# Rows of the last product 8 partitions apart, one VectorE copy and one output DMA, in a decode block on one core

## Chip, cores and metric

The kernel runs on one core of one Trainium2 chip. The metric is the device time of one execution in microseconds (us), as the median of several runs. The profile's span is about 2 us shorter than the time, because the two have different starts and ends. Spans are compared with spans here, and times with times.

## The reference, cut to what matters

The reference is one decode step of a transformer block for four sequences (B = 4): layer norm, attention over the last 2048 positions of a K and V cache, then layer norm and a gated MLP, each with a residual sum.

```python
# x: (4, 1, 1024); k_cache, v_cache: (4, 4, 8192, 128); wq: (1024, 4096); wo: (4096, 1024)
# w1, w3: (1024, 3584); w2: (3584, 1024); everything in bf16
h  = x + attention(layernorm(x), k_cache[:, :, -2048:], v_cache[:, :, -2048:], wq, wo)
h2 = h + (silu(layernorm(h) @ w1) * (layernorm(h) @ w3)) @ w2      # output: (4, 1, 1024)
```

There are only four rows of activations, so nearly all of the work is reading 55.6 MB of weights and cache. The output has 8 KB.

## The kernel before

The last product, `h @ w2` plus the residual, is what the change touches. The 1024 output columns are cut into JG = 4 slices of CG = 256. Slice `j` is computed by column group `j` of the TensorE array, so that four matmuls run side by side. Its four rows, one per sequence, stand in PSUM partitions 32j to 32j+3. The other partitions of each group of 32 are not used.

```python
# B = 4, JG = 4, QD = 32, CG = 256, IF = 7, P = 128
ident_f = const.tile([P, P], FP32)
nc.vector.tensor_copy(out=ident_f[:], in_=ident[:])
...
# the residual h1 (rows 32j+b) is put into the accumulator by an identity matmul
nc.tensor.matmul(y2_ps[:], lhsT=ident_f[:], rhs=h1[:], start=True, stop=False, skip_group_check=True)
... # gate, up, transposes of the gated product into hg_ps
hgT = act.tile([P, IF, JG, B], BF16)
nc.vector.tensor_copy(
    out=hgT[:], in_=hg_ps[:].rearrange("p i (j x) -> p i j x", j=JG)[:, :, :, :B]
)
for jf in range(JG):
    w2_t = loaded["w2"][jf]          # the last tile comes in pieces of 4, 2 and 1 chunks
    for i in range(IF):
        for j in range(JG):
            nc.tensor.matmul(
                y2_ps[QD * j : QD * j + B, :],
                lhsT=hgT[:, i, jf, :],
                rhs=w2_t[:, i, j * CG : (j + 1) * CG],
                start=False, stop=(jf == JG - 1 and i == IF - 1), skip_group_check=True,
            )

res = act.tile([P, CG], BF16)
nc.vector.tensor_copy(out=res[:, : CG // 2], in_=y2_ps[:, : CG // 2])
nc.scalar.copy(out=res[:, CG // 2 :], in_=y2_ps[:, CG // 2 :])
for j in range(JG):
    q = nc.sync if j % 2 == 0 else nc.scalar
    q.dma_start(out=out_flat[:, j * CG : (j + 1) * CG], in_=res[QD * j : QD * j + B, :])
```

Of the kernel before, what the change touches and what calls it, by code (L numbers as in the profile page):

```python
# [10 lines left out]
P = 128  # L11
# [3 lines left out]
BF16 = mybir.dt.bfloat16  # L15
FP32 = mybir.dt.float32
# [3 lines left out]
def kernel(  # L20
# [13 lines left out]
    nc = tc.nc  # L34

    B, _, D = A_x.shape
# [15 lines left out]
    out_flat = out.flatten_outer_dims()  # L52
# [9 lines left out]
    const = ctx.enter_context(tc.tile_pool(name="const", bufs=1))  # L62
    act = ctx.enter_context(tc.tile_pool(name="act", bufs=1))
# [3 lines left out]
    JG = 4  # L67
    QD = P // JG
    CQ = Hq * Dh // JG
    CG = D // JG  # L70
    CF = F // JG
    HF = CF // 2
    IF = CF // P
# [83 lines left out]
    ident = const.tile([P, P], BF16)  # L157
# [6 lines left out]
    for j in range(JG):  # L164
        nc.scalar.dma_start(
            out=x_q[QD * j : QD * j + B, :], in_=x_flat[:, j * CG : (j + 1) * CG]
# [7 lines left out]
    for c in range(2):  # L174
# [8 lines left out]
        out=xn[:], in0=x_sb[:], scalar1=mv[:, 0:1], scalar2=rstd[:, 0:1],  # L183
# [12 lines left out]

    qz = act.tile([P, B, Hkv * QD + REP], BF16)
    nc.vector.memset(qz[:], 0.0)
    ident_f = const.tile([P, P], FP32)
    nc.vector.tensor_copy(out=ident_f[:], in_=ident[:])  # L200

    sel = const.tile([P, RPO, RPO, P // RPO], BF16)
    ident_r = ident[:].rearrange("p (m r) -> p r m", r=RPO)
# [5 lines left out]
    for j in range(2, JG):  # L209
        nc.vector.tensor_tensor(  # L210
            out=same[:, 0, :], in0=same[:, 0, :], in1=ident[:, j * QD : (j + 1) * QD], op=ALU.add
# [6 lines left out]
    for kc in range(KC):  # L218
        wq_t = loaded["wq"][kc // KPC]
        for hf in range(CQ // 512):  # L220
            for g in range(JG):
# [3 lines left out]
                    lhsT=xnT[:, kc, :],  # L225
                    rhs=wq_t[:, kc % KPC, c0 : c0 + 512],
                    start=(kc == 0),
                    stop=(kc == KC - 1),
# [7 lines left out]
    for r in range(REP):  # L236
        nc.tensor.transpose(out=qt_ps[:, r, :], in_=q_sb[:, r * Dh : (r + 1) * Dh], identity=ident[:])
    nc.vector.tensor_copy(
        out=qz[:, :, : Hkv * QD].rearrange("p b (g z) -> p b g z", g=Hkv)[:, :, :, :REP],
        in_=qt_ps[:].rearrange("p r (g x) -> p x g r", g=Hkv)[:, :B, :, :],  # L240
# [24 lines left out]
    for u, (b, n) in enumerate(units):  # L265
        k_v = loaded["k"][b][:].rearrange("p (j d) -> p j d", d=Dh)
        kT = ktpool.tile([P, NJ, P], BF16, tag="kT")
        for t in range(NJ // TB):
            kt_ps = psA.tile([P, TB, P], BF16, tag=f"kt{nt % 4}")
            for jj in range(TB):  # L270
                nc.tensor.transpose(  # L271
                    out=kt_ps[:, jj, :], in_=k_v[:, n * NJ + t * TB + jj, :], identity=ident[:]
# [23 lines left out]
        out=Pm[:].rearrange("q (c jq) -> q jq c", jq=NSB), in_=scores_ps[:].rearrange("q (jq c) -> q jq c", jq=NSB),  # L296
# [22 lines left out]
    for b in range(B):  # L319
        v_t = loaded["v"][b]  # L320
        for g in range(Hkv):
            for j in range(NK):
                nc.tensor.matmul(  # L323
                    OT_ps[:, b, g * REP : (g + 1) * REP],
                    lhsT=v_t[:, g, j, :],
                    rhs=PT_sb[:, j, g * QD + b * REP : g * QD + (b + 1) * REP],
                    start=(j == 0),
                    stop=(j == NK - 1),
# [10 lines left out]
    for hh in range(RPO):  # L339
        nc.vector.tensor_copy(  # L340
            out=o4[hh * MP : (hh + 1) * MP, :, :, :].rearrange("p h r b -> p r h b"),
            in_=o4_ps[hh * MP : (hh + 1) * MP, :, :, hh, :],
# [7 lines left out]
    y2_ps = psB.tile([P, CG], FP32, tag="y2")  # L350
# [4 lines left out]
    for h4 in range(Hq // RPO):  # L355
        wo_t = loaded["wo"][h4 * RPO // HPC]
        for r in range(RPO):
            for j in range(JG):
                nc.tensor.matmul(  # L359
                    y_ps[QD * j : QD * j + B, :],  # L360
                    lhsT=o4[:, h4, r, :],
                    rhs=wo_t[:, h4 % (HPC // RPO), r, j * CG : (j + 1) * CG],
                    start=(h4 == 0 and r == 0),
                    stop=(h4 == Hq // RPO - 1 and r == RPO - 1),
# [5 lines left out]
    h1 = act.tile([P, CG], FP32)  # L370
# [20 lines left out]
        out=hn[:], in0=h1[:], scalar1=tot[:, 0:1], scalar2=rstd2[:, 0:1],  # L391
# [5 lines left out]
    for r in range(KPC):  # L397
# [3 lines left out]
        out=hnT[:], in_=hn_ps[:].rearrange("p r (j x) -> p j r x", j=JG)[:, :, :, :B]  # L401
    )

    nc.tensor.matmul(y2_ps[:], lhsT=ident_f[:], rhs=h1[:], start=True, stop=False, skip_group_check=True)


    def gate_up(kind, out_ps):
# [26 lines left out]
    hg_ps = psB.tile([P, IF, P], BF16, tag="tp")  # L434
    hg_v = hg[:].rearrange("q s c -> q (s c)").rearrange("q (p i) -> q i p", i=IF)
    for i in range(IF):
        nc.tensor.transpose(out=hg_ps[:, i, :], in_=hg_v[:, i, :], identity=ident[:])
    hgT = act.tile([P, IF, JG, B], BF16)
    nc.vector.tensor_copy(
        out=hgT[:], in_=hg_ps[:].rearrange("p i (j x) -> p i j x", j=JG)[:, :, :, :B]  # L440
    )


    for jf in range(JG):
        w2_t = loaded["w2"][jf]
        for i in range(IF):
            for j in range(JG):
                nc.tensor.matmul(  # L448
                    y2_ps[QD * j : QD * j + B, :],
                    lhsT=hgT[:, i, jf, :],  # L450
                    rhs=w2_t[:, i, j * CG : (j + 1) * CG],
                    start=False,
                    stop=(jf == JG - 1 and i == IF - 1),
                    skip_group_check=True,
                )

    res = act.tile([P, CG], BF16)
    nc.vector.tensor_copy(out=res[:, : CG // 2], in_=y2_ps[:, : CG // 2])  # L458
    nc.scalar.copy(out=res[:, CG // 2 :], in_=y2_ps[:, CG // 2 :])  # L459
    for j in range(JG):  # L460
        q = nc.sync if j % 2 == 0 else nc.scalar
        q.dma_start(out=out_flat[:, j * CG : (j + 1) * CG], in_=res[QD * j : QD * j + B, :])


# [28 lines left out]
```

## Time and profile before

| | before |
|---|---|
| time, median of 3 runs | 140.18 us (139.8 to 140.3) |
| span of the profiled run | 137.7 us |
| read from HBM | 55.59 MB, 404 GB/s over the span |
| last w2 data landed | 133.94 us |

The first lines are from the page of the kernel before: the span, the row of the 40 slices for the DMA engines (each digit is the busy share in tenths), and the chain that ended last, by line.

```profile
span 137.7 us, 2361 instructions
...
DMA  5999999999999999999999999999999999999950
...
DMA 61%; PE 22%; ACT 10%; DVE 2%; issue 2%; ACTq 0%
DMA w_t<-in_B_w_dram 42%; DMA k_t<-in_A_k_cache_dram 14%; PE kt_ps L271 11%; DMA wq_t<-in_A_wq_dram 5%; ACT kT L277 5%; PE scores_ps L256 5%; PE OT_ps L323 4%; ACT Pm L295 3%; DVE rmax L290 2%; PE pt_ps L309 1%; ACT L295 1%; PE y_ps L448 1%
```

The DMA engines are busy throughout, and the chain is mostly DMA. A change of the last steps can therefore gain only behind the last landing of weights.

The next lines are the timeline of the kernel before from there on. The columns are start and duration in us, then engine, line, operation and operands. The brackets give the idle time before an instruction and what ended it.

```profile
133.37 0.99 PE L448 MATMUL y_ps<-w_t,hgT 128*4 128x256 bf16 x12 [0.20 <-DMA w_t<-in_B_w_dram]
133.98 0.09 PEld L448 LDWEIGHTS <-hgT 128*4 128x4 bf16 x3 [0.32 <-issue]
134.41 0.29 DVE L458 CAST res<-y_ps 128x128 bf16<-128x128 f32 x1 [13.44 <-PE y_ps L448]
134.74 0.27 ACT L459 CAST res<-y_ps 128x128 bf16<-128x128 f32 x1 [30.90 <-DVE res L458]
135.03 0.66 SPq L462 DMA_DIRECT2D out_dram<-res  x2
135.03 0.62 ACTq L462 DMA_DIRECT2D out_dram<-res  x2
```

The ScalarE cast waited for the VectorE cast ("<-DVE res L458"), although it copies other columns, so the two halves came one after the other. Each queue then issued two DMAs. What follows them is not in the timeline but in the trace's records of landings and of the semaphore waits of SyncE, listed here in us of the span. A landing is the moment at which one DMA engine's share of a transfer counts as arrived.

```
before: last w2 landing 133.94 | first output issue 135.03
        the four output DMAs landed at 136.27  136.46  136.64  136.83 | end 137.72
        SyncE's closing waits released at 136.29  136.47  136.66  136.84  136.90
```

- "to issue" is from the last weight landing to the start of the first output issue (1.09 us here);
- "to landing" is from there to the last output landing (1.79 us);
- "to end" is from there to the end of the span (0.90 us).

Together the tail is 3.78 us.

### The profile page before, as it was taken

To read this page: it belongs to the slowest core of one execution; us is meant where nothing else is said; L and a number is where in the kernel's file an instruction comes from. 1 tells how busy PE (TensorE), PEld (TensorE's weight loads), DVE (VectorE), ACT (ScalarE), POOL (GpSimd) and SP (SyncE) were. 2 spreads that over 40 slices of the span, in tenths; PEclk is the share of its full clock that TensorE was granted. 3 is DMA by queue.
4 is the path that set the end of the run, shared out by engine and by line. 5 is a ranking of instruction groups with operands and counts; after the bars stand their busy time and mean duration, and the time that the engine had idled before them with its cause. 6 is when DMAs were issued, how large, how long until landed. Compare 5 with 4: busy or idle time off the path is not lost.

```text
span 137.7 us, 2361 instructions
## 1 busy us (share of the span) xinstructions
PE 73.3 (53%) x1057; PEld 43.4 (32%) x1057; DVE 37.0 (27%) x71; ACT 29.4 (21%) x29; POOL 0.7 (1%) x6
## 2 busy tenths in 40 slices
PE   0152254499898989400595759382244422654370
PEld 0111011296565656100595636220011110222220
DVE  6610000242343434530500181600008930300000
ACT  1200000125473737359440000000041000000000
POOL 2000000000000000000000000000000000000000
PEclk9999999999999999965555558965555555555555
DMA  5999999999999999999999999999999999999950
GB/s 159 453 401 438 438 409 447 438 409 443 424 416 406 419 421 424 419 425 428 431 424 428 424 442 417 437 416 450 413 446 416 446 421 433 433 421 441 398 236 2
DMA packets 6449, 55.74 MB, mean 405 GB/s; under 512 B 516, under 2 KB 548, under 8 KB 2856
## 3 DMA queue, kind: packets, MB, share of 16 engines
q1 hardware_dynamic: 6384, 55.58, 95.8%
q8 instruction: 8, 0.13, 0.3%
q10 hardware_dynamic: 56, 0.02, 0.1%
q14 instruction: 1, 0.01, 0.0%
HBM read 55.59 MB, written 0.01 MB: 404 GB/s over the span
## 4 chain that ended last, share of the span: by engine, by line
DMA 61%; PE 22%; ACT 10%; DVE 2%; issue 2%; ACTq 0%
DMA w_t<-in_B_w_dram 42%; DMA k_t<-in_A_k_cache_dram 14%; PE kt_ps L271 11%; DMA wq_t<-in_A_wq_dram 5%; ACT kT L277 5%; PE scores_ps L256 5%; PE OT_ps L323 4%; ACT Pm L295 3%; DVE rmax L290 2%; PE pt_ps L309 1%; ACT L295 1%; PE y_ps L448 1%; ACT PT_sb L315 0%; DVE res L458 0%; ACT res L459 0%
## 5 line engine op out<-in xcount | busy, mean ns | idle before, releaser
L277 ACT COPY kT<-kt_ps 128x1024 bf16<-128x1024 bf16 x16 | 15.9, 1013 | 15.0 <-PE kt_ps L271 15.0
L271 PE MATMUL kt_ps<-ident,k_t 128*128 128x128 bf16 x256 | 18.5, 235 | 0.9 <-DMA k_t<-in_A_k_cache_dram 0.9
L271 PEld LDWEIGHTS <-k_t 128*128 128x128 bf16 x256 | 16.4, 106 | 6.1 <-issue 4.9
L275 DVE COPY kT<-kt_ps 128x1024 bf16<-128x1024 bf16 x16 | 11.1, 692 | 18.1 <-PE kt_ps L271 18.1
L223 PE MATMUL q_ps<-wq_t,xnT 128*4 128x512 bf16 x64 | 7.5, 620 | 11.1 <-DMA wq_t<-in_A_wq_dram 11.1
L414 PE MATMUL u_ps<-w_t,hnT 128*4 128x448 bf16 x64 | 6.7, 568 | 10.4 <-DMA w_t<-in_B_w_dram 10.4
L414 PEld LDWEIGHTS <-hnT 128*4 128x4 bf16 x128 | 3.8, 104 | 24.4 <-issue 23.7
L256 PE MATMUL scores_ps<-kT,qz 128*32 128x512 bf16 x64 | 9.9, 609 | 3.0 <-ACT kT L277 3.0
L448 PE MATMUL y_ps<-w_t,hgT 128*4 128x256 bf16 x112 | 7.0, 410 | 6.7 <-DMA w_t<-in_B_w_dram 6.6
L414 PE MATMUL g_ps<-w_t,hnT 128*4 128x448 bf16 x64 | 6.1, 527 | 5.7 <-DMA w_t<-in_B_w_dram 5.5
L323 PE MATMUL OT_ps<-PT_sb,v_t 128*128 128x8 bf16 x256 | 7.4, 168 | 2.0 <-issue 1.8
L323 PEld LDWEIGHTS <-v_t 128*128 128x128 bf16 x256 | 7.3, 104 | 2.2 <-issue 2.0
L223 PEld LDWEIGHTS <-xnT 128*4 128x4 bf16 x64 | 2.0, 106 | 15.8 <-issue 15.4
L459 ACT CAST res<-y_ps 128x128 bf16<-128x128 f32 x1 | 0.3, 266 | 30.9 <-DVE res L458 30.9
L309 PE MATMUL pt_ps<-Dm,Pm 128*128 128x128 bf16 x16 | 1.9, 311 | 9.3 <-DVE Dm L302 9.3
L448 PEld LDWEIGHTS <-hgT 128*4 128x4 bf16 x112 | 3.7, 111 | 9.9 <-issue 7.8
L359 PE MATMUL y_ps<-wo_t,o_954 128*4 128x256 bf16 x128 | 5.1, 337 | 1.7 <-DVE y_ps L349 1.7
L427 DVE RECIPROCAL eg<-eg 128x896 f32<-128x896 f32 x1 | 5.8, 5752 | 0.0
L233 DVE TENSOR_SCALAR q_sb<-q_ps 128x512 bf16<-128x512 f32 x1 | 0.7, 692 | 16.9 <-PE q_ps L223 16.9
L234 ACT ACTIVATE q_sb<-q_ps 128x512 bf16<-128x512 f32 x1 | 0.6, 597 | 20.8 <-DVE q_sb L233 20.8
L295 ACT ACTIVATE Pm<-scores_ps,nmax 128x2048 bf16<-128x2048 f32 x1 | 4.8, 4784 | 0.0
L309 PEld LDWEIGHTS <-Pm 128*128 128x128 bf16 x16 | 1.6, 146 | 9.8 <-ACT Pm L295 9.8
(73 smaller groups left out, 42.4 us busy)
## 6 DMA issues: line engine op xcount, KB each, us to landing
w_t<-in_B_w_dram SPq DMA_DIRECT2D x11, 1792.0 KB, 27.9
wq_t<-in_A_wq_dram SPq DMA_DIRECT2D x4, 2048.0 KB, 11.6
k_t<-in_A_k_cache_dram SPq DMA_DIRECT2D x4, 2048.0 KB, 19.3
v_t<-in_A_v_cache_dram SPq DMA_DIRECT2D x4, 2048.0 KB, 36.8
wo_t<-in_A_wo_dram SPq DMA_DIRECT2D x4, 2048.0 KB, 22.8
w_t<-in_B_w_dram SPq DMA_DIRECT2D x1, 1024.0 KB
w_t<-in_B_w_dram SPq DMA_DIRECT2D x1, 512.0 KB, 29.3
w_t<-in_B_w_dram SPq DMA_DIRECT2D x1, 256.0 KB
```

Source lines behind the costliest of these rows:

```text
L223: nc.tensor.matmul(q_ps[QD * g : QD * g + B, hf * 512 : (hf + 1) * 512], lhsT=xnT[:, kc, :], rhs=wq_t[:, kc % KPC, c0 : c0 + 512], start=( ...
L256: nc.tensor.matmul(scores_ps[QD * g : QD * (g + 1), n * 512 : (n + 1) * 512], lhsT=qz[:, b, g * QD : (g + 1) * QD], rhs=kT_v[:, g, :, :], ...
L271: nc.tensor.transpose(out=kt_ps[:, jj, :], in_=k_v[:, n * NJ + t * TB + jj, :], identity=ident[:])
L275: nc.vector.tensor_copy(out=kT[:, t * TB : (t + 1) * TB, :], in_=kt_ps[:])
L277: nc.scalar.copy(out=kT[:, t * TB : (t + 1) * TB, :], in_=kt_ps[:])
L295: nc.scalar.activation(out=Pm[:].rearrange("q (c jq) -> q jq c", jq=NSB), in_=scores_ps[:].rearrange("q (jq c) -> q jq c", jq=NSB), func=A ...
L309: nc.tensor.matmul(pt_ps[:, jj, :], lhsT=Pm[:, (jb * JPB + jj) * P : (jb * JPB + jj + 1) * P], rhs=Dm[:], start=True, stop=True)
L323: nc.tensor.matmul(OT_ps[:, b, g * REP : (g + 1) * REP], lhsT=v_t[:, g, j, :], rhs=PT_sb[:, j, g * QD + b * REP : g * QD + (b + 1) * REP], ...
L359: nc.tensor.matmul(y_ps[QD * j : QD * j + B, :], lhsT=o4[:, h4, r, :], rhs=wo_t[:, h4 % (HPC // RPO), r, j * CG : (j + 1) * CG], start=(h4 ...
L414: nc.tensor.matmul(out_ps[QD * j : QD * j + B, hf, :HF], lhsT=hnT[:, k2, r, :], rhs=w_t[:, r, c0 : c0 + HF], start=(k2 == 0 and r == 0), s ...
L427: nc.vector.reciprocal(out=eg[:], in_=eg[:])
L448: nc.tensor.matmul(y2_ps[QD * j : QD * j + B, :], lhsT=hgT[:, i, jf, :], rhs=w2_t[:, i, j * CG : (j + 1) * CG], start=False, stop=(jf == J ...
```

## The change

The intent is to let one engine copy the result and one DMA store it. For that the four rows of each slice are spread over the 32 partitions of their group: row `b` of slice `j` goes to partition 32j+8b. All 16 rows are then exactly 8 partitions apart, and one access pattern with a partition step of 8 reaches them. The spreading is done by zero columns in the stationary operand, which becomes 32 columns wide.

```diff
-    ident_f = const.tile([P, P], FP32)
-    nc.vector.tensor_copy(out=ident_f[:], in_=ident[:])
+    RS = QD // B
+    spread = const.tile([P, JG, B, RS], FP32)
+    nc.vector.memset(spread[:], 0.0)
+    nc.vector.tensor_copy(
+        out=spread[:, :, :, 0], in_=ident[:].rearrange("p (j x) -> p j x", j=JG)[:, :, :B]
+    )
+    hgT = act.tile([P, IF, JG, B, RS], BF16)
+    nc.gpsimd.memset(hgT[:], 0.0)
...
-    nc.tensor.matmul(y2_ps[:], lhsT=ident_f[:], rhs=h1[:], start=True, stop=False, skip_group_check=True)
+    nc.tensor.matmul(
+        y2_ps[:], lhsT=spread[:].rearrange("p j b s -> p (j b s)"), rhs=h1[:],
+        start=True, stop=False, skip_group_check=True,
+    )
...
-    hgT = act.tile([P, IF, JG, B], BF16)
     nc.vector.tensor_copy(
-        out=hgT[:], in_=hg_ps[:].rearrange("p i (j x) -> p i j x", j=JG)[:, :, :, :B]
+        out=hgT[:, :, :, :, 0], in_=hg_ps[:].rearrange("p i (j x) -> p i j x", j=JG)[:, :, :, :B]
     )
...
-                    y2_ps[QD * j : QD * j + B, :],
-                    lhsT=hgT[:, i, jf, :],
+                    y2_ps[QD * j : QD * (j + 1), :],
+                    lhsT=hgT[:, i, jf, :, :].rearrange("p b s -> p (b s)"),
...
-    nc.vector.tensor_copy(out=res[:, : CG // 2], in_=y2_ps[:, : CG // 2])
-    nc.scalar.copy(out=res[:, CG // 2 :], in_=y2_ps[:, CG // 2 :])
-    for j in range(JG):
-        q = nc.sync if j % 2 == 0 else nc.scalar
-        q.dma_start(out=out_flat[:, j * CG : (j + 1) * CG], in_=res[QD * j : QD * j + B, :])
+    nc.vector.tensor_copy(out=res[:], in_=y2_ps[:])
+    nc.sync.dma_start(out=out_flat.rearrange("b (j c) -> j b c", j=JG), in_=res[0:P:RS, :])
```

On the DRAM side the 16 rows are in the order (slice, sequence). A step of one slice is 512 bytes and a step of one sequence is 2048 bytes.

## The prediction

> **What bounds the kernel.** The stream from HBM. The page's slices show the DMA engines at 9 tenths or more in 37 of 40, 404 GB/s over a 137.7 us span; the chain that ended last is 61% DMA, and from 104.07 to 133.33 us it is the weight loads alone. The engines wait for data (PE 53% busy; in the last product it idles 6.6 us in five waits for weight tiles). The change moves the same bytes in, so only the tail can change.
>
> **The tail before** (timeline, landing records): the last w2 piece lands at 133.94; its four matmuls run 133.98 to 134.39; VectorE casts half the result 134.41 to 134.71 (291 ns); ScalarE casts the other half only then, 134.74 to 135.01 (266 ns). Splitting bought no overlap. That agrees with the Trainium skill, "PSUM — Partial Sum Buffer", section on bank collisions: two engines are kept from touching one bank and quadrant together, and both halves lie in one bank. SyncE and ScalarE then issue two output DMAs each, 135.03 to 135.69. They land one after another at 136.27, 136.46, 136.64, 136.83. The closing barrier fills the rest to 137.72 (0.89 us).
>
> **What the change does, costed.**
> 1. No ScalarE cast; VectorE casts 256 columns. From the same engine reading PSUM at 128 columns (291 ns) and 512 (692 ns), an estimate for 256 is 425 ns. Done at 134.84 instead of 135.01: -0.17 us, on the path.
> 2. One DMA instead of four. The first of four took 1.24 us from issue to its last landing; the others cost 0.56 us more. One DMA has 16 rows of 512 B, four per engine instead of one (a packet takes about 28 ns: 0.08 us more): about -0.45 us, on the path. The skill's "DMA: Bandwidth & Descriptors", section "Issuing engines are not separate DMA queues", says that two issuing queues save only issue time; the landings 0.19 us apart agree.
> 3. The last product's stationary operand becomes 32 columns wide instead of 4. Weight loads of 32 columns took 93 ns, of 4 columns 80 to 85 at the same clock: 10 to 25 ns, paid once behind the last landing. Each matmul still streams 256 columns and the four column groups still overlap (28 matmuls in 1.66 us); the 2.6 us waits between tiles would hide more.
> 4. At the start: about 0.2 us more on VectorE and a GpSimd memset of 896 columns (about 1 us; a 128-column one took 0.20). The first big matmul waits for wq until 8.06 us, its transposed input is ready at 6.03: off the path. The strided hgT copy (217 ns before) may grow by tens of ns, hidden behind the wait for the second w2 tile.
>
> **Sum:** -0.17 - 0.45 + 0.02 = -0.6 us, 0.4%, about the run-to-run spread (139.8 to 140.3). From 140.18 I predict 139.6 us, 139.0 to 140.2 eight times in ten. Faster by over 2%: 0.01; within 2%: 0.98; slower: 0.01.
>
> **What would show each step:** no ScalarE cast, a VectorE cast near 425 ns; one output issue, landing 1.25 to 1.35 us later; the last w2 landing still at 133.5 to 134.3; the last product's matmuls within 3% of 7.0 us busy; span near 137.1.
>
> **What would make it wrong:** the single DMA landing late (fewer engines, rows apart slowing its reads); wide operands breaking the overlap of the column groups (over 2 us per tile); a shift in the stream's rate, where 1% is worth 1.3 us, more than the whole change; GpSimd's memset delaying VectorE by over 2 us at the start.

## The result and the profile after

| | before | change |
|---|---|---|
| time, median of 6 runs each | 140.00 us (139.75 to 140.40) | 139.85 us (139.76 to 140.08) |
| ratio, 95% interval | | 0.9987 (0.9967 to 1.0007) |
| span of the profiled run | 137.7 us | 138.0 us |
| last w2 landing | 133.94 us | 134.21 us |
| to issue + to landing + to end | 1.09 + 1.79 + 0.90 = 3.78 us | 0.95 + 1.79 + 1.09 = 3.83 us |

Ratios here and below are the mean time of one kernel's runs over that of the other's of the same rounds, so they are not quite the ratio of the medians. Executions over 1.5% slower than the fastest of the same kernel are left out of the means. The interval holds 1: no change of time is shown. The measured median lies inside the predicted range, but so does the time before (140.00 us), so this would have come out with no gain at all. The predicted gain of 0.6 us is nowhere in the tail.

The same lines of the page, for the changed kernel:

```profile
span 138.0 us, 2358 instructions
...
DMA  5999999999999999999999999999999999999940
...
DMA 61%; PE 22%; ACT 10%; DVE 2%; issue 2%; ACTq 0%
DMA w_t<-in_B_w_dram 41%; DMA k_t<-in_A_k_cache_dram 14%; PE kt_ps L278 11%; DMA wq_t<-in_A_wq_dram 5%; ACT kT L284 5%; PE scores_ps L263 5%; PE OT_ps L330 4%; ACT Pm L302 3%; DVE rmax L297 2%; PE pt_ps L316 1%; ACT L302 1%; PE y_ps L457 1%
```

The stream is the same, as predicted. The end of the timeline of the changed kernel:

```profile
133.62 1.04 PE L457 MATMUL y_ps<-w_t,hgT 128*32 128x256 bf16 x12 [0.20 <-DMA w_t<-in_B_w_dram]
134.25 0.11 PEld L457 LDWEIGHTS <-hgT 128*32 128x32 bf16 x3 [0.32 <-issue]
134.71 0.42 DVE L467 CAST res<-y_ps 128x256 bf16<-128x256 f32 x1 [13.06 <-PE y_ps L457]
135.16 0.69 SPq L468 DMA_DIRECT2D out_dram<-res  x1
```

One cast of 0.42 us and one issue are there, but that one issue took 0.69 us, as long as two issues before. The records behind it:

```
change: last w2 landing 134.21 | output issue 135.16
        its shares landed at 136.22 (the engines without a share)  136.88  136.90  136.91  136.95 | end 138.04
        SyncE's closing waits released at 136.96  137.03  137.09  137.16  137.22
```

Two things are seen before any experiment.

First, the single DMA landed 1.79 us after its issue began, exactly as late as the last of the four DMAs before. Its first packet started 1.28 us after the start of the issue; before, it was 0.76 us. The four late landings agree with the Trainium skill, "DMA: Bandwidth & Descriptors", section "Why a DMA increments its semaphore by 16 and not by 1": the number of DMA engines used is the largest one up to 16 that divides the slowest dimension of both sides, here 16 rows and 4 slices, so 4 engines.

Second, before, the four landings released four of SyncE's five closing waits one by one, and only one was left behind the last landing. After the change the first of the waits is for the one DMA, and the other four follow it at 0.06 to 0.07 us each. That is why the end takes 1.09 us instead of 0.90.

### The profile page after: what moved, and what is told of

It is laid out like the page before. It is cut to its first block, busy times and chain, and to the rows that moved or that the text cites. A ratio compares the mean times of both kernels' runs of the same rounds, so it can differ in the third digit from the quotient of the medians.

```text
span 138.0 us, 2358 instructions
## 1 busy us (share of the span) xinstructions
PE 73.8 (53%) x1057; PEld 44.6 (32%) x1057; DVE 37.7 (27%) x72; ACT 29.1 (21%) x28; POOL 1.5 (1%) x7
## 4 chain that ended last, share of the span: by engine, by line
DMA 61%; PE 22%; ACT 10%; DVE 2%; issue 2%; ACTq 0%
DMA w_t<-in_B_w_dram 41%; DMA k_t<-in_A_k_cache_dram 14%; PE kt_ps L278 11%; DMA wq_t<-in_A_wq_dram 5%; ACT kT L284 5%; PE scores_ps L263 5%; PE OT_ps L330 4%; ACT Pm L302 3%; DVE rmax L297 2%; PE pt_ps L316 1%; ACT L302 1%; PE y_ps L457 1%; ACT PT_sb L322 0%; DVE res L467 0%; DVE Dm L309 0%
## 5 line engine op out<-in xcount | busy, mean ns | idle before, releaser
L457 PE MATMUL y_ps<-w_t,hgT 128*32 128x256 bf16 x112 | 7.1, 414 | 6.6 <-DMA w_t<-in_B_w_dram 5.8
L457 PEld LDWEIGHTS <-hgT 128*32 128x32 bf16 x112 | 4.5, 135 | 9.2 <-issue 7.3
L366 PE MATMUL y_ps<-wo_t,o 128*4 128x256 bf16 x128 | 5.3, 344 | 1.7 <-DVE y_ps L356 1.7
L366 PEld LDWEIGHTS <-o 128*4 128x4 bf16 x128 | 3.5, 105 | 3.5 <-DVE y_ps L356 2.0
```

What stands on the lines that cost most here:

```text
L366: nc.tensor.matmul(y_ps[QD * j : QD * j + B, :], lhsT=o4[:, h4, r, :], rhs=wo_t[:, h4 % (HPC // RPO), r, j * CG : (j + 1) * CG], start=(h4 ...
L457: nc.tensor.matmul(y2_ps[QD * j : QD * (j + 1), :], lhsT=hgT[:, i, jf, :, :].rearrange("p b s -> p (b s)"), rhs=w2_t[:, i, j * CG : (j + 1 ...
```

## The experiments

Twelve runs were made, and each was also profiled. The tail is the most exact measure of what happens behind the last landing: in two profiles of the changed kernel it came to 3.83 us both times, while times of the same kernel spread over some tenths of a microsecond. It doesn't see a shift of the landing itself. The table gives all runs; the sections after it say what each was for.

| run | issue, each (us) | to issue | to landing | to end | tail | time / before in the same rounds (us) | ratio (95%) |
|---|---|---|---|---|---|---|---|
| before | 0.27 to 0.34 | 1.09 | 1.79 | 0.90 | 3.78 | | |
| change | 0.69 | 0.95 | 1.79 | 1.09 | 3.83 | 139.85 / 140.00 | 0.9987 (0.9967 to 1.0007) |
| a0_change_again | 0.69 | 0.95 | 1.79 | 1.09 | 3.83 | 139.84 / 139.70 | 1.0010 (0.9996 to 1.0023) |
| e1_four_dmas | 0.60 to 0.76 | 0.95 | 2.79 | 0.90 | 4.63 | 140.43 / 139.78 | 1.0050 (1.0036 to 1.0064) |
| e2_linear_rows (wrong) | 0.59 | 0.95 | 1.81 | 1.09 | 3.84 | 139.87 / 139.78 | 1.0009 (0.9996 to 1.0021) |
| e3_two_dmas | 0.63, 0.67 | 0.95 | 1.90 | 1.09 | 3.94 | 140.13 / 139.78 | 1.0027 (1.0014 to 1.0039) |
| e4_copy_alone | 0.27 to 0.34 | 0.93 | 1.79 | 0.90 | 3.62 | 139.54 / 139.78 | 0.9982 (0.9970 to 0.9995) |
| e5_last_semaphore | 0.70 | 0.95 | 1.80 | 0.84 | 3.58 | 140.45 / 139.72 | 1.0052 (1.0038 to 1.0067) |
| e6_dense_rows (wrong) | 0.80 | 0.95 | 1.90 | 1.09 | 3.94 | 140.01 / 139.72 | 1.0019 (1.0007 to 1.0032) |
| e7_dense_linear (wrong) | 0.36 | 0.95 | 1.42 | 1.09 | 3.45 | 139.47 / 139.72 | 0.9981 (0.9968 to 0.9994) |
| e8_step_two (wrong) | 0.61 | 0.95 | 1.83 | 1.09 | 3.86 | 139.89 / 139.72 | 1.0012 (0.9999 to 1.0026) |
| e9_scalar_copy | 0.27 to 0.34 | 0.87 | 1.79 | 0.89 | 3.56 | 139.48 / 139.70 | 0.9991 (0.9978 to 1.0004) |
| e10_last_semaphore_late | 0.67 | 0.95 | 1.79 | 0.84 | 3.58 | 139.68 / 139.70 | 1.0000 (0.9987 to 1.0012) |
| e11_rows_four_apart | 0.60 to 0.75 | 0.94 | 2.78 | 0.90 | 4.62 | 140.48 / 139.71 | 1.0053 (1.0036 to 1.0069) |

"Wrong" marks results that were wrong; all others were correct. In e10 the tail is counted from the last landing of w2 at 134.05 us, since one of the extra loads landed after it.

### a0_change_again: is the first profile typical?

The changed kernel was run again without an edit.

> The changed kernel once more, unchanged, on the chip of this call, for a second profile and a better ratio. Tail from the last weight landing to the end 3.83 us as in its first profile (0.95 to issue, 1.79 to landing, 1.09 to close), against 3.78 before; ratio of times 0.998 to 1.002.

The tail was 3.83 us again, with the same three parts, and the ratio was 1.0010. The last w2 landing was 134.03 us instead of 134.21, so that moment moves by some 0.2 us from run to run, and most of the 0.27 us by which it was later in the first profile is not an effect of the change. A small part may be: the landing was at 133.94 to 133.98 us in the three profiles with the old layout (before, e4, e9) and at 133.98 to 134.21 us in the ten with rows apart (all others but e5), with medians of 133.95 and 134.03 us. This shift of some 0.08 us lies before the tail, and its cause stays open.

### e1_four_dmas: why is the one DMA as slow as four?

My first theory, SHAPE, was that the two strides of the DRAM side make the issue slow. This run takes the second stride away and keeps the rows 8 partitions apart.

```diff
-    nc.sync.dma_start(out=out_flat.rearrange("b (j c) -> j b c", j=JG), in_=res[0:P:RS, :])
+    for j in range(JG):
+        q = nc.sync if j % 2 == 0 else nc.scalar
+        q.dma_start(out=out_flat[:, j * CG : (j + 1) * CG], in_=res[QD * j : QD * (j + 1) : RS, :])
```

> The changed kernel, but its one output DMA cut into four of four rows each, two on SyncE and two on ScalarE as before; rows stay 8 partitions apart. Theory SHAPE (the single DMA is slow to issue because its DRAM side steps through two strides, slices and batches): each issue is back at 0.27 to 0.34 us, first landing about 1.25 us and last landing about 1.8 us after the first issue, closing part 0.9 us again. From the last weight landing to the end: 0.95 + 1.8 + 0.9 = 3.65 us, 0.13 under the kernel before. Rival ROWS (16 rows, four per DMA engine, cost it): the same here. Rival DISTANCE (rows 8 partitions apart are slow to fetch): packets and landings stay late, first landing 1.5 us or more after issue. Time: within 0.2% of the changed kernel, so the trace decides, not the clock.

SHAPE fell. These are the instructions that write or read the result tile, for the kernel before and then for this run. The numbers after "x2:" are the shortest, median and longest duration in ns.

```profile
L462 SPq DMA_DIRECT2D out_dram<-res x2: 276/306/337, 135.0 to 135.4; - x2
L462 ACTq DMA_DIRECT2D out_dram<-res x2: 274/291/308, 135.0 to 135.3; - x2
```

```profile
L470 SPq DMA_DIRECT2D out_dram<-res x2: 687/721/755, 135.0 to 135.8; - x2
L470 ACTq DMA_DIRECT2D out_dram<-res x2: 602/650/698, 135.0 to 135.7; - x2
```

The DRAM side, the number of rows and the queues are the same in the two kernels. Only the partitions of the rows differ: neighbours before, every eighth here. Each issue takes more than twice as long, each queue has two of them in a row, and the last landing comes 2.79 us after the first issue instead of 1.79. The time is 0.5% longer than before, which is outside its noise. The rival DISTANCE was right that the partition step costs, but not in how: the packets themselves are not slow (25 to 33 ns each before and after the change); it is the issue that takes longer.

### e2_linear_rows and e3_two_dmas: rows, strides or step?

In e2 the one DMA writes its rows in one stride of DRAM. The order of the output is then wrong.

```diff
-    nc.sync.dma_start(out=out_flat.rearrange("b (j c) -> j b c", j=JG), in_=res[0:P:RS, :])
+    nc.sync.dma_start(out=out_flat.rearrange("b (j c) -> (b j) c", j=JG), in_=res[0:P:RS, :])
```

> Wrong order of the result on purpose: one DMA of the same 16 rows, but its DRAM rows follow each other in one stride of 512 bytes. SHAPE: issue 0.33 us instead of 0.69, last landing 1.25 to 1.35 us after issue instead of 1.79, time about 0.4 us (0.3%) under the changed kernel. ROWS, as far as it means 16 rows to generate: issue stays at 0.69 (if it means four rows per engine it may fall too, since 16 rows can now be dealt to 16 engines; the landing count tells). DISTANCE: landing stays at 1.7 us or more. Reference comparison must fail.

In e3 two DMAs of eight rows each keep both strides and the step.

```diff
-    nc.sync.dma_start(out=out_flat.rearrange("b (j c) -> j b c", j=JG), in_=res[0:P:RS, :])
+    for k in range(2):
+        q = nc.sync if k == 0 else nc.scalar
+        q.dma_start(
+            out=out_flat[:, 2 * k * CG : 2 * (k + 1) * CG].rearrange("b (j c) -> j b c", j=2),
+            in_=res[2 * QD * k : 2 * QD * (k + 1) : RS, :],
+        )
```

> The changed kernel with two output DMAs of eight rows, one on SyncE, one on ScalarE, each still with two strides on the DRAM side. SHAPE: each issue still takes 0.6 to 0.7 us though it has half the rows, side by side; last landing about 1.8 to 2.0 us after issue, no gain over one DMA. ROWS: issue falls to about 0.45 to 0.5 us and the last landing to about 1.5 us. DISTANCE: no change of issue, landing as in the changed kernel.

In e2 the issue fell only from 0.69 to 0.59 us and the landing stayed at 1.81 us, although the 16 rows were now dealt to 16 engines (16 late landings in the records instead of 4). So four rows per engine were not the only cost either. In e3 half the rows took 0.67 and 0.63 us, so the issue does not scale with the rows. SHAPE happened to expect the numbers of e3 rightly, but e1 and e2 had already taken it down as the only cause.

### e6, e7 and e8: each cause alone

The partition step and the second DRAM stride were now tested apart. All three runs read the wrong partitions or write in the wrong order.

```diff
 e6_dense_rows    in_=res[0 : JG * B, :]              out "b (j c) -> j b c"     (16 neighbours, two strides)
 e7_dense_linear  in_=res[0 : JG * B, :]              out "b (j c) -> (b j) c"   (16 neighbours, one stride)
 e8_step_two      in_=res[0 : 2 * JG * B : 2, :]      out "b (j c) -> (b j) c"   (every second, one stride)
```

> Wrong result on purpose: the changed kernel, the one DMA reads 16 neighbouring partitions instead of every eighth; DRAM side with its two strides as in the change. My SHAPE theory fell in the first runs (four-row DMAs without a second stride took 0.60 to 0.76 us each when their rows lie 8 apart). New theory STEP (a partition step other than 1 on the SBUF side alone makes an issue slow): issue 0.28 to 0.40 us, first packet 0.76 us after issue, last landing 1.25 to 1.4. Rival EITHER (a second stride on the DRAM side or a step on the SBUF side, each sends the issue down the slow way; the 16-row linear one took 0.59 and the loads of the K cache with more dims took 0.6): issue 0.55 to 0.7 us, last landing 1.65 or more.

> Wrong result on purpose: neighbouring partitions and one linear stride of DRAM. STEP and EITHER both: issue 0.28 to 0.35 us, last landing about 1.25 to 1.35 us, 0.45 to 0.55 under the changed kernel; tail from last weight landing about 3.3 us; time about 0.35% under the changed kernel. Rival ROWS (16 rows are slow to issue however they lie): issue 0.55 or more, last landing 1.7 or more.

> Wrong result on purpose: 16 rows two partitions apart, one linear stride of DRAM. STEP: as with a step of 8, issue 0.59 us, last landing 1.8. Rival DISTANCE, as far as it means how far apart the rows lie: between the dense one and the one of 8, issue near 0.35 to 0.45 us.

The issue of the one DMA, from the instructions of the result tile, in the order e6, e7, e8:

```profile
L468 SPq DMA_DIRECT2D out_dram<-res x1: 795/795/795, 135.0 to 135.0; - x1
```

```profile
L468 SPq DMA_DIRECT2D out_dram<-res x1: 355/355/355, 135.0 to 135.0; - x1
```

```profile
L468 SPq DMA_DIRECT2D out_dram<-res x1: 612/612/612, 134.9 to 134.9; - x1
```

With the changed kernel and e2 this makes a square for one DMA of 16 rows of 512 bytes (issue / last landing after the start of the issue, us):

| | one DRAM stride | two DRAM strides |
|---|---|---|
| 16 neighbouring partitions | 0.36 / 1.42 (e7) | 0.80 / 1.90 (e6) |
| every second partition | 0.61 / 1.83 (e8) | |
| every eighth partition | 0.59 / 1.81 (e2) | 0.69 / 1.79 (change) |

EITHER was right in kind, though the 0.80 us of e6 is above its 0.55 to 0.7, and STEP as the only cause fell with e6. Each of the two alone makes the issue slow and moves the landing by about 0.4 to 0.5 us; both together cost no more than one. A step of 2 costs as much as a step of 8, so the distance does not matter. And 16 rows as such are cheap: e7 landed after 1.42 us, a little over the 1.25 to 1.35 expected and near the 1.32 us (1.24 + 0.08) that my prediction used for the change. Its time was 0.19% under before, about half of the gain that the change was meant to bring. What in the hardware makes the difference, these runs don't show.

One rival is left in the square: with one DRAM stride the rows went to 16 engines, with two strides to 4 (16 and 4 late landings), so the second stride never came alone. The loads of the kernel before settle this for the issue, and I could have read it before I predicted. These are the instructions of two of its lines: the K cache (two strides in DRAM over the rows) and the weights wq (one stride). Both load 128 rows of 16 KB, and both land on 16 engines. For the landing of the output the rival stays open.

```profile
L95 SPq DMA_DIRECT2D k_t<-in_A_k_cache_dram x4: 593/608/615, 8.0 to 10.0; - x4
```

```profile
L89 SPq DMA_DIRECT2D wq_t<-in_A_wq_dram x4: 328/406/424, 0.7 to 2.4; - x4
```

The number of strides is not a complete rule, however. The load of `x_sb` has four neighbouring partitions and one stride of 2 KB, and its issue took 0.55 to 0.58 us in every run; it is the first DMA that ScalarE issues, and no run tells whether that is why. The first V load has its second DRAM stride inside each partition's row; it took 0.59 to 0.61 us right behind the K loads, but 0.40 us in e5, where it came 1.6 us after them.

### e4_copy_alone and e9_scalar_copy: the copy without the rest

Here the kernel before keeps its layout and its four DMAs and takes only one copy.

```diff
-    nc.vector.tensor_copy(out=res[:, : CG // 2], in_=y2_ps[:, : CG // 2])
-    nc.scalar.copy(out=res[:, CG // 2 :], in_=y2_ps[:, CG // 2 :])
+    nc.vector.tensor_copy(out=res[:], in_=y2_ps[:])        # e4_copy_alone
+    nc.scalar.copy(out=res[:], in_=y2_ps[:])               # e9_scalar_copy
```

> The kernel before with one part of the change alone: VectorE copies all 256 columns, ScalarE none; four output DMAs as before. All theories: copy 0.42 us, issue starts 0.14 to 0.17 us earlier after the last weight landing than before (0.92 to 0.95 instead of 1.09), the rest as before (1.8 to the last landing, 0.9 to close): 3.63 us from the last weight landing to the end instead of 3.78. Time 0.1% under before, inside the noise of the clock.

> The kernel before with ScalarE copying all 256 columns and VectorE none; four output DMAs as before. From ScalarE's 266 ns at 128 columns and 597 at 512, an estimate for 256 is 376 ns, 0.05 under VectorE's 425. So the issue starts 0.88 us after the last weight landing and the tail is 3.57 us; time 0.1 to 0.2% under before, not to be told from the copy by VectorE alone.

The end of the timeline of e4, and then the copy in e9:

```profile
134.42 0.42 DVE L458 CAST res<-y_ps 128x256 bf16<-128x256 f32 x1 [13.44 <-PE y_ps L448]
134.88 0.66 SPq L461 DMA_DIRECT2D out_dram<-res  x2
134.88 0.62 ACTq L461 DMA_DIRECT2D out_dram<-res  x2
```

```profile
134.45 0.37 ACT L458 CAST res<-y_ps 128x256 bf16<-128x256 f32 x1 [30.56 <-PE y_ps L448]
```

Both came out as expected: 3.62 and 3.56 us of tail against 3.78. The copy is the part of the change that gains, and it needs no new layout. In time, e4 is 0.18% under before, with an interval that leaves 1 out. For e9 the medians say 0.16%, but one of its five runs took 139.95 us, and its interval holds 1. The two were not run in the same rounds, so which is better is not shown by time.

Why ScalarE waited for VectorE in the kernel before is not shown. The prediction put it down to the shared PSUM bank. Two other pairs of copies stand in the same trace:

```profile
24.46 0.69 DVE L233 TENSOR_SCALAR q_sb<-q_ps 128x512 bf16<-128x512 f32 x1 [16.86 <-PE q_ps L223]
25.18 0.60 ACT L234 ACTIVATE q_sb<-q_ps 128x512 bf16<-128x512 f32 x1 [20.82 <-DVE q_sb L233]
...
67.34 0.69 DVE L313 CAST PT_sb<-pt_ps 128x512 bf16<-128x512 f32 x1 [0.77 <-PE pt_ps L309]
67.77 0.59 ACT L315 CAST PT_sb<-pt_ps 128x512 bf16<-128x512 f32 x1 [1.69 <-PE pt_ps L309]
```

In the first pair the engines read two halves of 512 columns of one tile, `q_ps`, and ScalarE waited as well. In the second they read different tiles, and ScalarE began at 67.77 us, before VectorE ended at 68.03. So in this program the wait goes with a shared PSUM tile. Whether two half copies overlap when the halves are in two tiles was not run.

### e5_last_semaphore and e10_last_semaphore_late: the longer end

In these traces the DMAs take their completion semaphores in turn from eight numbers, and SyncE waits for them in a fixed order at the end. In the changed kernel the output DMA has the first in this order. Four more small loads, whose data nobody reads, give it the last one.

```diff
+    x_more = act.tile([B, 4, CG], BF16)
+    for j in range(4):
+        nc.scalar.dma_start(out=x_more[:, j, :], in_=x_flat[:, j * CG : (j + 1) * CG])
```

In e5 these lines stand at the start, behind the loads of `x_q`. In e10 they stand before `gate_up("w3", u_ps)` and are issued by SyncE, behind the last weight load.

> The changed kernel with four more small loads at the start, which are never read; they only shift the output DMA from the first of the semaphores that SyncE waits for at the end to the last. Theory CLOSE (the four staggered landings of before hid SyncE's other closing waits; a single landing on the first semaphore makes them follow it, 65 ns each): from the last landing to the end 0.83 to 0.90 us instead of 1.09, everything else as in the changed kernel. Rival (the closing part is 0.2 us longer because one DMA's landing is acknowledged later): stays at 1.09. Time 0.1% under the changed kernel at most.

> The mended form of the run with four more loads: in that one they stood at the start, one of them waited for the semaphore of the first weight load, and ScalarE with it, so that the first large product began 3.5 us later. Here they are issued behind the last weight load, when their semaphores are free. Theory CLOSE: first large product at about 8.1 us as in the changed kernel, last weight landing 134.0 to 134.3, closing part 0.84 instead of 1.09, tail 3.57 us; time 0.25 us (0.2%) under the changed kernel. If the closing part is 0.84 and the time does not move, the last landing has moved instead.

The closing part fell to 0.84 us in both, as CLOSE had it: in e10 SyncE's first four closing waits were released 0.88 to 1.07 us before the landing, and only one was left behind it. So the order of the waits costs 0.26 us (1.09 - 0.84, from unrounded values) in the changed kernel.

In time, e5 was 0.5% slower nevertheless. The lines of its timeline show what was delayed; the second fence has the weight loads of wq in the changed kernel:

```profile
2.67 5.61 ACTq L171 DMA_DIRECT2D x_more<-in_A_x_dram  x4
...
6.58 2.06 SPq L89 DMA_DIRECT2D wq_t<-in_A_wq_dram  x3
...
8.30 1.28 ACT L183 ACT_TABLE_LOAD   x1 [8.30 <-DMA wq_t<-in_A_wq_dram]
...
11.62 1.88 PE L234 MATMUL q_ps<-wq_t,xnT 128*4 128x512 bf16 x16 [0.27 <-DVE xnT L195]
```

```profile
0.73 2.17 SPq L89 DMA_DIRECT2D wq_t<-in_A_wq_dram  x4
```

Two things were late. The fourth extra load had to wait for the semaphore of the first weight load. ScalarE waited with it, its square root for the layer norm came late, and the first large product began at 11.62 instead of 8.08 us. And the extra loads had taken the next semaphores in turn: SyncE's second load of wq got that of an `x_q` load, waited for it and was issued at 6.58 instead of 1.18 us. The last w2 landing moved by 0.75 us, from 134.21 to 134.96. The late weight loads suffice for that: in the first 12 us the DMA engines moved 323 instead of 351 GB/s, 0.34 MB less, which at the 432 GB/s of the changed kernel from 12 to 30 us is an estimated 0.78 us. That the late product adds to it is not shown. In e10 the first product began at 8.11 us and w2 landed at 134.05. Its median was 139.68 us, against 139.84 for the changed kernel of the same rounds; the intervals of their ratios to before overlap, so a gain is shown by the tail (0.25 us) and only suggested by the time (0.16 us).

### e11_rows_four_apart: the step once more, and a copy that tripled

Two open points: whether a step of 4 behaves like the others, and why VectorE's strided copy of `hgT` grew from 217 to 652 ns. The rows were put 4 partitions apart; the zero columns fill the stationary operand to 32 columns as before, so only the distance of the writes changes.

```diff
 against e1_four_dmas:
-    RS = QD // B
-    spread = const.tile([P, JG, B, RS], FP32)
+    RS, RB = 4, QD // 4
+    spread = const.tile([P, JG, RB, RS], FP32)
-        out=spread[:, :, :, 0], ...
+        out=spread[:, :, :B, 0], ...
-    hgT = act.tile([P, IF, JG, B, RS], BF16)
+    hgT = act.tile([P, IF, JG, RB, RS], BF16)
-        out=hgT[:, :, :, :, 0], ...
+        out=hgT[:, :, :, :B, 0], ...
-        q.dma_start(out=out_flat[:, j * CG : (j + 1) * CG], in_=res[QD * j : QD * (j + 1) : RS, :])
+        q.dma_start(out=out_flat[:, j * CG : (j + 1) * CG], in_=res[QD * j : QD * j + B * RS : RS, :])
```

> The run with four DMAs of four rows, with the rows 4 partitions apart instead of 8; the stationary operand stays 32 columns wide. Two questions. (1) Issue: if any step other than 1 sends it the slow way, each of the four issues again takes 0.60 to 0.76 us and the tail from the last weight landing is 4.6 us; if distance matters, less. (2) The strided copy of hgT, which grew from 217 to 652 ns (the prediction had tens of ns) when its writes came to stand 16 bytes apart: the Trainium skill, 'SBUF — State Buffer', section 'Specifications (TRN2)', speaks of 16-byte lines that need two hits each for full bandwidth. If that is it, writes 8 bytes apart take 220 to 260 ns; if any stride is slow, the copy stays near 650.

The issues took 0.60 to 0.75 us and the tail was 4.62 us: a step of 4 is as slow as one of 8. The copy of `hgT`, in the instructions of its tile, for the kernel before, the change and this run:

```profile
L439 DVE COPY hgT<-hg_ps x1: 217/217/217, 120.8 to 120.8; 128x112 bf16<-128x112 bf16 x1
```

```profile
L448 DVE COPY hgT<-hg_ps x1: 652/652/652, 121.0 to 121.0; 128x112 bf16<-128x112 bf16 x1
```

```profile
L448 DVE COPY hgT<-hg_ps x1: 392/392/392, 120.8 to 120.8; 128x112 bf16<-128x112 bf16 x1
```

The writes stand 2, 16 and 8 bytes apart. Neither expectation held: 8 bytes is between the other two, not at full speed. The lines of 16 bytes that the Trainium skill, "SBUF — State Buffer", section "Specifications (TRN2)", describes give the direction, since sparser writes are slower, but not the size; whether the lines are the reason, no run shows. None of this is on the critical path, because the next tile of w2 is waited for anyway.

## Why the prediction was right or wrong, point by point

**The bound and the verdict were right.** The stream takes the time up to about 134 us, nothing in the change moves it by more than about 0.1 us, and the time stays within 2%. The range held the median of 139.85 us, which took no insight: 139.0 to 140.2 us held the time before as well, and the largest term of the sum was wrong. Whether 139.85 is better than before at all is not shown: the ratios of the two measurements, 0.9987 and 1.0010, lie on both sides of 1.

**Step 1, the copy, was right.** "An estimate for 256 is 425 ns"; it took 424 ns. With the wide operand of step 3, the part up to the issue was to become 0.15 us shorter and became 0.14 us shorter (1.090 to 0.948). The ScalarE cast had waited for VectorE's before, and e4 shows that the copy alone gains 0.16 us of tail. The place in the Trainium skill that the prediction named, "PSUM — Partial Sum Buffer", section "PSUM bank collisions raise a hardware error", says that two engines must not meet in one bank and quadrant. The wait fits that, but ScalarE waited in the same way for the other half of `q_ps` (e4, above), so the bank is not shown to be its reason, and no run here let the two engines collide.

**Step 2, "one DMA instead of four", was wrong, and it was the largest term.** I took the first of four DMAs (1.24 us), added 0.08 us for its packets and wrote "about -0.45 us, on the path". It measured 0.00: 1.79 us before and after. The step that failed was the assumption that the new DMA is issued like the old ones. Its SBUF side steps by 8 partitions and its DRAM side has two strides, and the square of runs shows that with either of these the issue goes from 0.36 to 0.59 us or more and the landing from 1.42 to between 1.8 and 1.9 us. With neither of them (e7, whose result is wrong), 0.37 us of the expected 0.45 us are there. The list of what could go wrong had "rows apart slowing its reads": the step did matter, but in the issue and not in the reads.

**The closing part, "0.89 us", was treated as a constant and was not one.** It grew by 0.195 us, because the four landings, spread over 0.56 us, had let three of SyncE's five closing waits pass before the last landing, and a single landing on the first semaphore lets none pass. e10 brings it to 0.84 us by the order of the semaphores alone.

**The sum, in unrounded parts:** predicted -0.17 - 0.45 + 0.02 = -0.60 us; measured -0.142 - 0.005 + 0.195 = +0.05 us of tail.

**Step 3, the wide stationary operand, was right.** From the last landing to the end of the last matmul it took 0.448 us instead of 0.424, so 24 ns more, against the 10 to 25 predicted. The column groups still overlap: 28 matmuls took 1.69 us instead of 1.66.

**Step 4 was right about the start and wrong in one size.** GpSimd's memset took 0.85 us and the first large product still began at 8.08 us. The copy of `hgT` grew by 435 ns, not by "tens of ns"; it was hidden, as predicted.

**Versions with a shorter tail than both kernels.** In tail, e9 (3.56 us), e10 (3.58) and e4 (3.62) are all shorter than before (3.78) and than the change (3.83). By time, of the correct ones, only e4 is below before with an interval that leaves 1 out, by 0.18%. It is also the smallest edit: one copy instead of two.

## What to carry to other kernels

Fewer DMAs are not by themselves a faster end: compare the access patterns as well as the count, and look in the same trace at what an issue of the planned pattern costs (here, output DMAs of neighbouring partitions and one DRAM stride 0.27 to 0.36 us, those with a partition step or two strides 0.59 to 0.80). Cut a tail into its parts (last data in, issue, last landing, end) and cost each, the closing waits included; where each part repeats within hundredths of a microsecond, it decides what the clock cannot, but only for what lies inside the tail. When two engines copy two parts of one PSUM tile, see whether the second waited for the first; here, where it did, one copy by one engine was shorter.

## What the Trainium skill lacked or had wrong

- "DMA: Bandwidth & Descriptors": no section that I found ties the time of an issue to the pattern. The runs show 0.27 to 0.36 us for output DMAs of neighbouring partitions and one DRAM stride, and 0.59 to 0.80 us with a partition step of 2, 4 or 8 or with two DRAM strides. The issue of `x_sb` (0.55 to 0.58 us, neighbouring partitions, one stride) doesn't fit and is not explained.
- The same page, section "Rules for kernel authors", says to coalesce many small transfers into one large one. Here four transfers of 2 KB became one of 8 KB and landed no sooner (1.79 us both); with neighbouring rows and one stride it did (1.42 us in e7, whose result is wrong).
- The same page, section "Latency and other measured facts", gives about 600 ns to the first byte for DMAs of SyncE and ScalarE. Here the first output packet came 0.76 us after the start of the issue in before and 0.85 us in e7, and 1.25 to 1.39 us after it in the runs with a step or with two strides.
- The same page, section "Anatomy of one DMA — SWDGE (gpsimd) path", has a fixed cost of about 2.0 us for GpSimd's DMAs. For one issued by SyncE or ScalarE the runs show 1.24 us from issue to the last landing, with four rows of 512 bytes.
- No page that I found has the closing waits of SyncE: 0.06 to 0.07 us each in series behind one landing, 0.26 us in all between the best and the worst order.
- "SBUF — State Buffer", section "Specifications (TRN2)": at least two hits per 16-byte line are said to be needed for full bandwidth. VectorE's copy of 112 columns took 217 ns with writes 2 bytes apart, 392 ns at 8 bytes and 652 ns at 16 bytes, so two writes per line (8 bytes) were not enough for full speed, if the lines are what slows the copy.
